# Keeping the loads of q, k, v and of layer one's raw weights in the source's order on the load queue

## The chip, the cores and the metric

The kernel runs on one core of a Trainium2 chip. The metric is the device time of one execution in microseconds (us); three timed runs of the kernel before are given, and one more execution was profiled. The engines are named as the profile names them: PE is the matrix engine (PEld its weight loads), ACT the scalar engine, DVE the vector engine, POOL GpSimd, and SPq the queue of the sync engine, on which this kernel issues all of its DMAs.

## The reference

Inputs are q, k and v in f32, 4 batches of 8 heads, 576 positions, 64 columns a head, and the weights of two layers in f64.

```python
scores = q @ k.T / sqrt(64)
Dmat   = where(i >= j, gamma[h] ** (i - j), 0)       # gamma = 1 - 2 ** (-5 - h)
x      = (scores * Dmat) @ v                          # heads side by side: 2304 x 512
h      = x @ w_in1                                    # 512 -> 2048
x      = where(h > 0, h, exp(min(h, 0)) - 1) @ w_out1 # 2048 -> 512
h      = maximum(x @ w_in2, 0)
out    = (h * h) @ w_out2
```

## The kernel before, in words

**Attention.** Because of the decay matrix the attention is computed as a recurrence over positions. The 2304 tokens are cut into chunks of at most 128 positions of one batch; chunk 0 to 3 make up the first token block, chunk 4 to 8 the second, 9 and 10 the third, 11 to 14 the fourth, 15 to 19 the fifth. A chunk has three loads on SPq, q, k and v (`load_chunk`, L204), a scaling of q and k (`scale_chunk`, L214, on POOL for the chunks of block 0 that are loaded first, on DVE otherwise) and three pieces of work: the transposes (L239, copied out by ACT on L244), the scores (L252, masked by DVE on L255), and the values (L267 with the state `st` of the chunk before, L271 with v, then L281 and L287 or L289 for the new state). Chunk 1 to 3 live in space that later belongs to weights; all others share two buffers for each of q, k and v. So the loads of chunk 6 wait until chunk 4 is done with its buffers, those of chunk 7 until chunk 5 is, and so on; k and v are free once the new state's matmuls (L281) have read them.

**Weights.** Both layers are computed in three matmuls for each product (L130 to L132), from a high and a low f32 part. A weight arrives as raw f64, 512 KB for each of the 32 units of a layer (a unit is one 128-wide slice of w_in or of w_out; L145 and L150 in `load_raw`). `to_f32` turns it into f32 with two ACT operations (L160, L161) and four of DVE (L162, L163, L164, L167); `split_w` makes the two parts (ACT L126, DVE L127). Layer one's raw tile lies in the space in which the split weight comes to lie, so each of the 32 units has a place of its own.

**Order in the source.** `load_next` for chunk 0 and 1, raw units 0 and 1, chunk 2 and 3. Then the pieces of chunk 0 to 3 in a written order, with `w1_to(n)` after each: it has n units split, n + 1 converted, and raw units asked for up to `AHEAD` beyond the converted ones. Chunk 4 is loaded after chunk 0's values, chunk 5 after chunk 2's. Then come the steps: step i multiplies one block by one slice of w_in (`up`), and two steps later by the slice of w_out (`down1`). Steps 0 to 5 belong to block 0, steps 6 to 11 to block 1. Each of the steps 0 to 4 first holds the three pieces of one of the chunks 4 to 8, and with a chunk's values the loads of the chunk two further on; then it calls `w1_to` with the limits 8, 9, 11, 12 and 14.

**Order on the engines.** The program isn't issued in the source's order. A list scheduler goes over all instructions with a simulated clock and issues on each engine what is ready first, earlier in the source before later among the ready. What an engine's list holds is fixed when the kernel is compiled, and each engine then works down its own list. A load of a raw unit of layer one is ready from the beginning, as soon as its place is free; a chunk's load is ready only when its buffers are free. In the same way a list can be tied: an issue-order edge says that one instruction of an engine stands behind another in its list, without a semaphore.

Of the kernel before, what the change touches and what calls it, by code (L numbers as in the profile page):

```python
# [18 lines left out]
P = 128  # L19
# [6 lines left out]
LAG = 2  # L26
WARM = 3

AHEAD = 6


GROUPS = ((0, 6), (6, 11), (11, 16))
# [66 lines left out]
def tile_kernel(ctx: ExitStack, tc, q, k, v, w_in1, w_out1, w_in2, w_out2, cst, out):  # L99
    nc = tc.nc  # L100
# [36 lines left out]
    def load_raw(layer, which, f):  # L137
        w = ((w_in1, w_out1), (w_in2, w_out2))[layer][which].bitcast(I32)
        if layer == 0:

            t = wp.tile([P, DM, 2], I32, tag=f"w{which}_{f}", name="raw")
        else:
            t = raw_p.tile([P, DM, 2], I32, tag="raw", name="raw")
        if which == 0:
            nc.sync.dma_start(  # L145
                out=t.rearrange("p (k f) t -> p k (f t)", k=KC),
                in_=w[:, 2 * f * P:2 * (f + 1) * P].rearrange("(k p) f -> p k f", p=P),
            )
        else:
            nc.sync.dma_start(out=t.rearrange("p c t -> p (c t)"), in_=w[f * P:(f + 1) * P, :])  # L150
        raws[layer, which, f] = t

    def to_f32(u):
# [38 lines left out]
    def load_chunk(ch):  # L192
        b, s, n = ch
        ts = []
        if ch in aside:
            tags = [f"w{i % 2}_{NF - 1 - 2 * aside.index(ch) - i // 2}" for i in range(4)]
            ts4 = [wp.tile([P, 2, DM], F32, tag=t, name="spare") for t in tags]
            spare[ch] = [t[:, i] for t in ts4 for i in range(2)]
        for i, (src, nm) in enumerate(((q, "q"), (k, "k"), (v, "v"))):
            if ch in aside:  # L200
                t = spare[ch][i].rearrange("s (h d) -> s h d", h=H)
            else:
                t = n_p.tile([P, H, D], F32, tag=nm, name=nm)
            nc.sync.dma_start(out=t[:n], in_=src[b, :, s:s + n, :].rearrange("h s d -> s h d"))  # L204
            ts.append(t)
        nat[ch] = ts

# [185 lines left out]
    def load_next():  # L393
        if at["load"] < len(chunks):
            load_chunk(chunks[at["load"]][0])
            at["load"] += 1
# [20 lines left out]
    def step(name, limit, todo_, work):  # L417
        if at[name] < min(limit, len(todo_)):
            work(todo_[at[name]])
            at[name] += 1  # L420
# [11 lines left out]
    def w1_run(n):  # L432
        while at["split"] < min(int(n), len(w1)):
            while at["raw"] < min(at["f32"] + AHEAD, len(w1)):
                step("raw", 99, w1, lambda u: load_raw(*u))
            step("split", at["f32"], w1, split_w)
            step("f32", at["raw"], w1, to_f32)
# [6 lines left out]
    for u in w1[:2]:  # L444
        load_raw(*u)
        at["raw"] += 1
# [17 lines left out]
    for i, (layer, blk, f) in enumerate(steps):  # L464
        def mid():
            for of, (lo, hi) in SPREAD.items():
                if lo <= i < hi:
                    need = 3 * len(blocks[of])
                    for _ in range((i - lo + 1) * need // (hi - lo) - (i - lo) * need // (hi - lo)):
                        attn_step()  # L470
            if at["split"] < len(w1):
                w1_to(units1(i))
            elif layer == 0 and i >= SHARED and at["f322"] < min(len(w2), units2(i)):

                step("park", at["f322"], w2, park_w)
                with tc.issue_after(mark[0]):
                    step("f322", at["raw2"], w2, to_f32)
                while at["raw2"] < min(len(w2), at["f322"] + 2):
                    step("raw2", 99, w2, lambda u: load_raw(*u))
# [19 lines left out]
        if (layer, f) == (0, 1) and blk == NB - 1 or (layer, f) == (1, LAG) and blk < NB - 1:  # L499
            n = blk + 1 if layer else 0  # L500
# [30 lines left out]
```

## Time and profile before

| what | us |
|---|---|
| median of three timed runs | 938.24 |
| lowest and highest of them | 931.86 and 939.58 |
| the profiled execution | 935.93 |
| its span, first to last instruction | 934.2 |
| granted PE clock, mean over the span | 0.982 |

The span is what the trace shows; 1.7 us of the profiled execution lie around it. The median of the timed runs is 2.3 us above the profiled execution. A share of busy time near 1 for PE does not say that its clock was full: the granted clock is a column of its own, 1.00 for 2.4 GHz and 0.50 for 1.2 GHz.

### The profile page before, as it was taken

The page shows a single profiled execution, that of the slowest core. Times are in us where ns is not written, and L with a number is a line of the kernel's source. Part 1 is how long each engine was busy: PE and PEld are TensorE (multiplying, and loading weights), DVE is VectorE, ACT ScalarE, POOL GpSimd, SP SyncE. Part 2 cuts the span into 40 slices and gives each one's busy share as a digit, 9 for nine tenths or more (in the row PEclk, how much of TensorE's full clock was granted, in tenths as well). Part 3 has the DMA queues.
Part 4 walks back from the last instruction along what each step waited for, and adds up shares of the span by engine and source line. Part 5 has one row for each costly group of instructions (what it writes and reads, how often), then busy time and mean ns, then how long its engine had stood idle before and what let it go on. Part 6 is the DMA issues. An engine that isn't in the chain of part 4 may idle for free.

```text
span 934.2 us, 12422 instructions
## 1 busy us (share of the span) xinstructions
PE 904.7 (97%) x4934; PEld 751.4 (80%) x4934; DVE 508.7 (54%) x890; ACT 422.7 (45%) x770; POOL 9.1 (1%) x12
## 2 busy tenths in 40 slices
PE   7897899999999999999999999999999999999997
PEld 5775788777788987888788888888888988888886
DVE  5886887787668788776787632222223332223222
ACT  3663577665555666555677532222222222222221
POOL 3000000000000000000000000000000000000000
PEclk9798899999999999999999999999999999999999
DMA  9994333102437757434844520010003030001001
GB/s 244 295 369 103 67 93 101 63 29 91 135 97 230 214 138 215 124 126 168 293 136 147 169 91 1 1 66 25 1 1 135 1 113 1 1 1 45 1 1 45
DMA packets 97081, 97.47 MB, mean 104 GB/s; under 512 B 59264, under 2 KB 77824, under 8 KB 96512
## 3 DMA queue, kind: packets, MB, share of 16 engines
q1 hardware_dynamic: 97024, 96.69, 34.2%
q8 instruction: 38, 0.62, 0.3%
q14 instruction: 19, 0.16, 0.0%
HBM read 69.94 MB, written 26.74 MB: 103 GB/s over the span
## 4 chain that ended last, share of the span: by engine, by line
PE 89%; SPq 3%; DMA 3%; DVE 2%; ACT 1%; issue 1%; DVEq 0%
PE h L130 14%; PE acc L130 14%; PE h L132 14%; PE h L131 14%; PE acc L131 14%; PE acc L132 13%; SPq L204 2%; PE ps_o L271 2%; PE ps_s L252 1%; PE ps_o L267 1%; PE ps_t L239 1%; DMA f<-w2s 1%; DMA k<-in_k_dram 1%; DMA raw<-in_moe_w_out_dram 1%; PE ps_u L281 1%
## 5 line engine op out<-in xcount | busy, mean ns | idle before, releaser
L130 PE MATMUL h<-x,w 128*128 128x512 f32 (+1 forms) x640 | 240.0, 376 | 3.9 <-DVE t L317 3.5
L132 PE MATMUL h<-x,w 128*128 128x512 f32 (+1 forms) x640 | 237.5, 371 | 0.0
L131 PE MATMUL h<-x,w 128*128 128x512 f32 (+1 forms) x640 | 237.5, 371 | 0.0
L321 DVE SCALAR_TENSOR_TENSOR t<-h,t 128x512 f32<-128x512 f32 (+1 forms) x80 | 51.0, 638 | 230.0 <-ACT t L319 230.0
L319 ACT ACTIVATE t<-h 128x512 f32<-128x512 f32 (+1 forms) x80 | 44.4, 555 | 237.2 <-PE h L132 237.2
L130 PEld LDWEIGHTS h<-x,w 128*128 128x128 f32 x640 | 121.9, 191 | 27.5 <-DVE t L317 4.1
L132 PEld LDWEIGHTS h<-x,w 128*128 128x128 f32 x640 | 121.8, 190 | 20.9 <-DVE w L127 0.2
L131 PEld LDWEIGHTS h<-x,w 128*128 128x128 f32 x640 | 122.0, 191 | 20.5
L126 ACT CAST g<-t 128x512 fp32r<-128x512 f32 (+1 forms) x160 | 92.5, 578 | 99.7 <-DVE t L321 52.1
L127 DVE TENSOR_TENSOR g<-t,g 128x512 fp32r<-128x512 f32 (+1 forms) x160 | 101.8, 636 | 64.5 <-ACT g L126 58.3
L131 PE MATMUL acc<-g,w 128*128 128x512 f32 (+1 forms) x320 | 118.3, 371 | 0.0
L132 PE MATMUL acc<-g,w 128*128 128x512 f32 (+1 forms) x320 | 117.0, 370 | 0.0
L130 PE MATMUL acc<-g,w 128*128 128x512 f32 (+1 forms) x320 | 114.0, 377 | 0.9 <-ACT w L126 0.9
L130 PE MATMUL acc<-w,g 128*128 128x512 f32 x288 | 112.2, 390 | 0.0
L131 PE MATMUL acc<-w,g 128*128 128x512 f32 x288 | 112.2, 390 | 0.0
L132 PE MATMUL acc<-w,g 128*128 128x512 f32 x288 | 111.6, 389 | 0.0
L312 ACT ACTIVATE t<-h 128x512 f32<-128x512 f32 (+1 forms) x80 | 44.4, 555 | 87.2 <-PE h L132 83.3
L316 DVE SCALAR_TENSOR_TENSOR t<-e,t 128x512 f32<-128x512 f32 (+1 forms) x80 | 50.8, 636 | 54.8 <-ACT t L314 54.7
L130 PEld LDWEIGHTS acc<-g,w 128*128 128x128 f32 x320 | 59.5, 188 | 12.5 <-ACT w L126 1.1
L132 PEld LDWEIGHTS acc<-g,w 128*128 128x128 f32 x320 | 60.2, 188 | 10.2
L131 PEld LDWEIGHTS acc<-g,w 128*128 128x128 f32 x320 | 60.3, 188 | 9.9 <-issue 0.2
L132 PEld LDWEIGHTS acc<-w,g 128*128 128x128 f32 x288 | 54.1, 188 | 11.4
(65 smaller groups left out, 933.0 us busy)
## 6 DMA issues: line engine op xcount, KB each, us to landing
raw<-in_moe_w_in_dram SPq DMA_DIRECT2D x32, 512.0 KB, 6.5
raw<-in_moe_w_out_dram SPq DMA_DIRECT2D x32, 512.0 KB, 6.0
x2s<-x SPq DMA_DIRECT2D x16, 512.0 KB, 4.0
w2s<-f SPq DMA_DIRECT2D x32, 256.0 KB, 2.3
x<-x2s SPq DMA_DIRECT2D x4, 2048.0 KB, 8.3
f<-w2s SPq DMA_DIRECT2D x32, 256.0 KB, 2.7
out_dram<-o SPq DMA_DIRECT2D x18, 256.0 KB, 2.3
parts<-part SPq DMA_DIRECT2D x8, 512.0 KB, 3.4
```

Source lines behind the costliest of these rows:

```text
L126: nc.scalar.copy(pair_hi, src)
L127: eng.tensor_tensor(out=pair_lo, in0=src, in1=pair_hi.bitcast(F32), op=ALU.subtract)
L130: nc.tensor.matmul(ps, l_hi, r_hi, start=first, stop=False)
L131: nc.tensor.matmul(ps, l_hi, r_lo, start=False, stop=False)
L132: nc.tensor.matmul(ps, l_lo, r_hi, start=False, stop=last)
L204: nc.sync.dma_start(out=t[:n], in_=src[b, :, s:s + n, :].rearrange("h s d -> s h d"))
L239: nc.tensor.transpose(ps[:, p, :n], t[:n, 2 * p:2 * p + 2, :].rearrange("s h d -> s (h d)"), ident[:n, :n])
L271: nc.tensor.matmul(ps[e * D:(e + 1) * D, p, :n], vn[:n, 2 * p + e, :], live[e][:n, p, :n], start=not s, stop=True, skip_group_check=True,)
L312: nc.scalar.activation(t, h, AF.Relu, scale=-1.0)
L316: nc.vector.scalar_tensor_tensor(out=t, in0=e, scalar=1.0, in1=t, op0=ALU.add, op1=ALU.mult)
L319: nc.scalar.activation(t, h, AF.Relu)
L321: nc.vector.scalar_tensor_tensor(out=t, in0=h, scalar=0.0, in1=t, op0=ALU.max, op1=ALU.mult)
```

## The change

Each load of q, k and v, and each load of a raw unit of layer one, gets an issue-order edge to the instruction that stands just before it in the source on the same queue, whatever that is (`tc.keep_in_program_order`; the edge carries no semaphore). The raw loads of layer two, the stores and the loads of parked values get none. `AHEAD` is 4 in place of 6, so that `w1_to(n)` asks for raw units up to n + 4 in place of n + 6.

```diff
-AHEAD = 6
+AHEAD = 4
...
         if which == 0:
-            nc.sync.dma_start(
+            i = nc.sync.dma_start(
                 out=t.rearrange("p (k f) t -> p k (f t)", k=KC),
...
         else:
-            nc.sync.dma_start(out=t.rearrange("p c t -> p (c t)"), in_=w[f * P:(f + 1) * P, :])
+            i = nc.sync.dma_start(out=t.rearrange("p c t -> p (c t)"), in_=w[f * P:(f + 1) * P, :])
+        if layer == 0:
+
+            tc.keep_in_program_order(i)
         raws[layer, which, f] = t
...
-            nc.sync.dma_start(out=t[:n], in_=src[b, :, s:s + n, :].rearrange("h s d -> s h d"))
+            tc.keep_in_program_order(
+                nc.sync.dma_start(out=t[:n], in_=src[b, :, s:s + n, :].rearrange("h s d -> s h d"))
+            )
```

## Rows read from the trace of the kernel before

**Rows 1.** The page's second part: busy tenths and granted clock in 40 slices.

```profile
PE   7897899999999999999999999999999999999997
...
PEclk9798899999999999999999999999999999999999
```

**Rows 2.** Windows: PE, PEld, DVE, ACT, POOL busy us; granted clock, DMA share, GB/s.

```profile
38.30:115.90 77.60, 66.63 (x471) 53.71 (x469) 62.28 (x116) 42.76 (x80) 0.00 (x0) 0.91 0.65 188
...
38.30:74.00 35.70, 32.72 (x211) 25.76 (x210) 31.30 (x59) 22.51 (x41) 0.00 (x0) 1.00 1.00 327
40.00:60.00 20.00, 18.75 (x126) 15.16 (x127) 19.10 (x38) 15.00 (x28) 0.00 (x0) 1.00 1.02 355
```

**Rows 3.** Timeline of PE, 46 to 123 us; in brackets idle us before and its releaser.

```profile
46.57 0.68 PE L271 MATMUL ps_o<-P,v 64*64 64x64 f32 x16
...
73.91 0.63 PE L239 MATMUL ps_t<-cs,q 128*128 128x128 f32 x4 [1.28 <-DVE q L214]
...
80.26 2.08 PE L267 MATMUL ps_o<-qT,st 128*128 128x128 f32 x8 [3.35 <-DVE P L255]
...
85.45 0.50 PE L130 MATMUL h<-x,w 128*128 128x512 f32 x1 [0.35 <-ACT w L126]
...
115.86 0.48 PE L130 MATMUL h<-x,w 128*128 128x512 f32 x1
...
122.58 0.50 PE L130 MATMUL h<-x,w 128*128 128x512 f32 x1
```

**Rows 4.** Timeline of DVE, 78 to 81 us.

```profile
78.92 0.69 DVE L214 TENSOR_TENSOR k<-k,cs 128x512 f32<-128x512 f32 x1 [1.58 <-DMA k<-in_k_dram]
79.53 1.28 DVE L255 TENSOR_TENSOR P<-ps_s,cs 128x512 f32<-128x512 f32 x2
```

**Rows 5.** The chain that ended last, in order of time, at 72 us.

```profile
72.03 6.87 DMA k<-in_k_dram
```

**Rows 6.** Timeline of SPq, 21 to 64 us: start and length of DMA issues.

```profile
21.13 0.73 SPq L204 DMA_DIRECT2D q<-in_q_dram  x1
...
25.01 1.69 SPq L145 DMA_DIRECT2D raw<-in_moe_w_in_dram  x1
...
39.66 0.79 SPq L150 DMA_DIRECT2D raw<-in_moe_w_out_dram  x1
...
59.96 1.25 SPq L145 DMA_DIRECT2D raw<-in_moe_w_in_dram  x1
61.31 2.27 SPq L204 DMA_DIRECT2D q<-in_q_dram  x1
63.68 3.66 SPq L204 DMA_DIRECT2D k<-in_k_dram  x1
```

**Rows 7.** Windows in which PE or its clock falls, columns as in rows 2.

```profile
80.00:85.00 5.00, 4.74 (x40) 4.43 (x40) 1.48 (x4) 0.70 (x2) 0.00 (x0) 0.50 0.00 0
...
90.00:110.00 20.00, 16.40 (x146) 13.54 (x143) 17.95 (x36) 8.71 (x18) 0.00 (x0) 0.83 0.32 66
280.00:285.00 5.00, 2.56 (x22) 2.37 (x23) 5.00 (x11) 1.31 (x3) 0.00 (x0) 0.81 0.86 273
455.00:465.00 10.00, 7.84 (x28) 6.02 (x27) 7.69 (x14) 6.20 (x11) 0.00 (x0) 0.83 0.74 246
```

**Rows 8.** Raw loads of L145 up to 75 us: us to landing.

```profile
DMA to landing us min/median/max: 5.1/9.2/12.0
```

**Rows 9.** Timeline of ACT: conversions of raw units 5 and 8 begin.

```profile
31.00 0.65 ACT L160 ACTIVATE raw<-raw 128x512 int32<-128x512 uint32 x1
...
47.57 0.68 ACT L160 ACTIVATE raw<-raw 128x512 int32<-128x512 uint32 x1
```

**Rows 10.** Waits of SPq up to 130 us: sum, times, longest.

```profile
SPq L204 <- PE ps_u L281: 27.8, 4, 9.0
```

**Rows 11.** The page's DMA issues: KB each, median us to landing, whole span.

```profile
raw<-in_moe_w_in_dram SPq DMA_DIRECT2D x32, 512.0 KB, 6.5
...
k<-in_k_dram SPq DMA_DIRECT2D x13, 256.0 KB, 4.5
```

## The prediction

> **What bounds the kernel now.** I read the slices of the page first, then windows of the span, then PE's timeline where a window was not full, and from there back over DVE to the load queue. PE is the bound on the whole; nearly every slice after the fifth is full and at full clock [rows 1]. What can move the time is therefore what PE loses, as idle time or by a low clock. It loses most between 38.3 us, where step 0 begins, and 115.9 us, where step 6 does: 77.6 - 66.6 = 11.0 us idle, and at a mean clock of 0.91 another 0.09 x 66.6 = 6.0 us [rows 2]. The change works on the loads of just this stretch, so 17 us are at stake.
>
> The largest single hole is a late load. PE waits 1.28 us for the scaling of chunk 6's q and 3.35 us for chunk 6's mask [rows 3]. The mask was not late by itself: DVE had it behind the scaling of chunk 7's k, and that waited for its DMA [rows 4], which was issued at 72.03 us and took 6.87 us [rows 5]. Why so late: chunk 4's values, the last that hold buffers for chunk 6, begin at 46.57 us and last 0.68 [rows 3], yet chunk 6's q goes out at 61.31 and its k at 63.68 us, because raw loads stand in front, 19 of them, the one at 39.66 us the first and the one at 59.96 us the last [rows 6]. They are 19 x 0.524 = 10 MB, and the DMA engines are full (share 1.00 up to 74 us [rows 2]). None of the 19 is wanted soon: they are the units from 12 on, and the conversion of unit 8 begins at 47.57 us [rows 9].
>
> **The change part by part.**
>
> *Chunk loads no longer behind the raw loads.* In the source chunk 6's loads follow chunk 4's values in step 0, and the raw units from 11 on follow them. So chunk 6's q and k go out when their buffers are free, some 14 us earlier, and chunk 7's when chunk 5's state is done, with few raw loads beside them (a k landed in 4.5 us in the median of the span [rows 11], against 6.87 here). Then DVE isn't held in L214, and the 1.28 and the 3.35 us go. The clock fell to 0.50 after this hole [rows 7]; that cost half of 4.74 us, 2.4 us, and goes with it. Sum: 7.0 us.
>
> *The rest of the stretch.* From 90 to 110 us PE loses 3.6 us idle and 0.17 x 16.4 = 2.8 us by the clock [rows 7]. Here chunk 7 and 8 go through their chains of transposes, copies, scores, mask and values with only steps 4 and 5 beside them, since steps 1 to 3 were used up while chunk 6 was waited for. With the loads on time each chunk lies beside its own step. That could bring back all 6.4 us or nothing; what is late next is DVE. It works 62.28 us of these 77.6. While it was fed, from 38.3 to 74 us, it was busy for 31.30 of 35.70 us (88%), and in its fullest 20 us for 19.10 (95.5%) [rows 2]. The same work at these rates takes 62.28 / 0.88 = 71.0 or 62.28 / 0.955 = 65.2 us, so the whole stretch can gain 6.6 to 12.4 us. I take a third of the 6.4, 2.1 us: 7.0 + 2.1 = 9.1 us is near the middle of what DVE allows.
>
> *Four units ahead.* Raw units 5 and 6 change places with chunk 4's loads, which held the queue from 21.13 to 25.01 us [rows 6]. So unit 5 goes out at 23 us; with the 9.2 us that raw loads took here [rows 8] it lands at 32.2, 1.2 us after its conversion began in the kernel before [rows 9]. The cost lies between 0 (DVE's backlog hides it, or the load is quicker with less beside it) and 1.2 us; I take 1.2. From unit 11 on the raw loads stand behind the loads of chunk 6 and later ones. `w1_to` asks for a unit 4 units before it is converted, at 1.4 units a step 2.9 steps; steps 0 to 3 took 85.45 - 38.3 = 47.2 us [rows 3], so the lead is some 30 us. The queue's longest wait for a chunk's buffers was 9.0 us [rows 10], with a landing of 9.2 us [rows 8] 18.2 us: covered. I cost it at nothing; without this cover it is the second rival.
>
> *Later stages.* After unit 31 the edges hold q, k and v behind stores and behind raw loads of layer two. A q that used to go out ahead of its k then stands beside it; DVE scales k after q anyway, which hides it. PE's losses at 280 to 285 us (2.44 us idle, 0.19 x 2.56 = 0.5 us by the clock) and at 455 to 465 us (2.16 us idle, 0.17 x 7.84 = 1.3 us) [rows 7] end with other waits than that for a chunk's load. But the scheduler draws up every list anew, so such a hole may vanish or come a second time: 3 us either way at the one, 3.5 at the other. I take 0.
>
> *Sum.* 935.9 (the profiled execution) - 7.0 - 2.1 + 1.2 = 928.0 us. The timed median, 938.24, is 2.3 us above the profiled execution and the lowest run 4.1 us below it; the mean of all four is 936.4, so I make no correction.
>
> *A rule that speaks against the change.* SPq stood for 27.8 us in four waits for a chunk's buffers [rows 10], and nothing was issued in them. The Trainium skill, "DMA: Bandwidth & Descriptors", section "Anatomy of one DMA — SWDGE (gpsimd) path", says that DMA engines don't wait on semaphores; the issuing sequencer waits before it dispatches. The trace agrees with it for this queue. By that rule a chunk load whose buffers aren't free would hold back each raw load behind it, and the sum would be the second rival's.
>
> **The rivals.** About 1% is what a measurement of this kernel can tell from no change: 9.4 us, or 928.9 us on the faster side.
>
> First, DVE takes the load's place: the loads come early, but PE next waits for the queue of conversions, scalings and masks. For it speaks that DVE was busy for 19.1 of 20 us [rows 2]; against it that PE still got 18.75 of these, and that DVE worked 1.48 of the 5 us after the hole [rows 7]. The gain is then DVE's lower bound less the late unit, 6.6 - 1.2 = 5.4 us, and less than that if a hole of 3 us comes later: 930.5 to 933.5, say 932 us.
>
> Second, on the slower side: the wait moves to the raw loads. The place is SPq in steps 1 to 4, where raw units from 11 on stand behind chunk 6 to 9. ACT's and DVE's lists are drawn up with simulated landing times; where these are too early, a conversion stands in front of masks and scalings and waits for its raw load. The price: three chunks, each with one raw load waited for by its whole landing, 6.5 us [rows 11], are 19.5 us, less the 7.9 that the change otherwise gives: 935.9 + 11.6, some 947 us. It decides from where the lead falls below 18.2 us, that is for steps under 18.2 / 2.9 = 6.3 us. Step 6 was nearly that short (122.58 - 115.86 = 6.7 us), steps 0 to 3 took 11.8 us each [rows 3]. Against it: no ACT operation waited for a raw load in this stretch before.
>
> Third, the order changes but nothing follows: chunk 7's k still waits for chunk 5's state, and if the pieces of chunk 5 keep their place, the hole only moves: 936 us.
>
> Fourth, more gain: the 17 us of the stretch less 2 us for copies that stay, and half of the 7.4 us lost at 280 and 455 us, 18.7 in all: 917 us.
>
> **How the numbers follow.** Forecast 0.47, spread over 921 to 934 us with two thirds below 928.9; more gain 0.14; DVE 0.13; no effect 0.06; slower 0.20. Faster by over 1%: 0.31 + 0.14 = 0.45. Within 1%: 0.16 + 0.13 + 0.06 = 0.35. Slower: 0.20. The range from 918 to 944 us leaves out half of the fourth rival and half of the second, 0.17; the likeliest case alone has 921 to 934 us.
>
> **What would show it.** On SPq, chunk 6's q soon after chunk 4's values and before raw unit 11, and the last raw units far later than 60 us. A DMA share well under 1.00 between 45 and 75 us. No wait of DVE L214 for q or k above 1 us, step 6 near 107 us, and a granted clock of 1.00 from 75 to 85 us. For the second rival, waits of ACT L160 for raw loads. The prediction is wrong if step 6 begins as late as before, or if it begins earlier and the time is given back in new holes after 200 us.

## The result, and the profile after

The changed kernel takes 925.33 us (median of 4 runs, 924.72 to 926.99), the kernel before 937.13 (4 runs, 931.86 to 939.58): a ratio of 0.9884, 95% interval 0.9839 to 0.993. A later series gave 926.67 (6 runs, 923.43 to 928.73) and a ratio of 0.9903, interval 0.9878 to 0.9929. The profiled execution took 924.95 us, of which the span is 923.2, so 11.0 us less than the span of before, 934.2.

The page, span, PE's slices with the granted clock, and the raw loads' row of the DMA issues, answers to [rows 1, 11]:

```profile
span 923.2 us, 12432 instructions
...
PE   7898999999999999999999999999999999999997
...
PEclk9899899999999999999999999999999999999999
...
raw<-in_moe_w_in_dram SPq DMA_DIRECT2D x32, 512.0 KB, 5.3
```

The clock's digits in the second and the fourth slice are one higher, the eight in the fifth stays. A raw load lands in 5.3 us in the median, not 6.5. Next the load queue, start and length of issues; it answers to [rows 6]. Lines have moved: L208 is the load of a chunk.

```profile
23.00 1.23 SPq L145 DMA_DIRECT2D raw<-in_moe_w_in_dram  x1
...
38.26 0.37 SPq L208 DMA_DIRECT2D q<-in_q_dram  x1
38.73 0.55 SPq L208 DMA_DIRECT2D k<-in_k_dram  x1
45.76 0.37 SPq L208 DMA_DIRECT2D v<-in_v_dram  x1
46.18 0.57 SPq L145 DMA_DIRECT2D raw<-in_moe_w_in_dram  x1
...
59.64 0.37 SPq L208 DMA_DIRECT2D k<-in_k_dram  x1
...
150.01 0.50 SPq L150 DMA_DIRECT2D raw<-in_moe_w_out_dram  x1
```

Chunk 6's q goes out at 38.26 us (61.31 before) and its k at 38.73 (63.68), ahead of raw unit 11 at 46.18; chunk 7's k goes out at 59.64 (72.03 before), and raw loads still go out at 150 us. PE's timeline, to hold against [rows 3]: chunk 4's matmuls with v, waits of chunk 5, transposes of chunk 6, its first values, chunk 8's passage, and the first matmul of step 8 (the prediction calls it step 6).

```profile
45.04 0.68 PE L276 MATMUL ps_o<-P,v 64*64 64x64 f32 x16
...
47.24 0.66 PE L244 MATMUL ps_t<-cs,k 128*128 128x128 f32 x4 [0.93 <-ACT qT L249]
48.57 2.09 PE L257 MATMUL ps_s<-qT,kT 64*128 64x128 f32 x16 [0.68 <-ACT kT L249]
...
67.13 0.60 PE L244 MATMUL ps_t<-cs,q 128*128 128x128 f32 x4
...
75.46 1.05 PE L272 MATMUL ps_o<-qT,st 128*128 128x128 f32 x8
...
91.24 0.44 PE L244 MATMUL ps_t<-cs,q 64*128 64x64 f32 x4 [0.74 <-DVE st L292]
91.87 0.46 PE L244 MATMUL ps_t<-cs,k 64*128 64x64 f32 x4 [0.20 <-DVE x L127]
92.79 0.68 PE L257 MATMUL ps_s<-qT,kT 64*64 64x64 f32 x16 [0.46 <-ACT kT L249]
94.11 1.97 PE L272 MATMUL ps_o<-qT,st 128*128 128x64 f32 x8 [0.64 <-DVE P L260]
...
108.55 0.50 PE L130 MATMUL h<-x,w 128*128 128x512 f32 x1
```

The q goes out 23.0 us earlier than before, and ahead of chunk 4's values. Chunk 4 is the last of its batch: it makes no new state, so its q and k are done with after its transposes, and only the load of v (45.76 us) waits for its values (45.04 + 0.68 us). The same transposes in the kernel before:

```profile
37.95 0.46 PE L239 MATMUL ps_t<-cs,q 64*128 64x64 f32 x4
...
39.00 0.46 PE L239 MATMUL ps_t<-cs,k 64*128 64x64 f32 x4
```

So there the q stood some 23 us behind the raw loads (61.31 - 38.4), not the 14 that the prediction counts from chunk 4's values.

Chunk 6's transposes begin 6.8 us earlier and wait for nothing, and its values, which stood 3.35 us for the mask, begin at 75.46 in place of 80.26 without a wait. The step that begins at 108.55 began at 115.86. Windows, columns as in [rows 2]:

```profile
37.62:108.59 70.97, 65.82 (x467) 53.38 (x465) 61.02 (x115) 41.78 (x78) 0.00 (x0) 0.93 0.48 129
37.62:67.10 29.48, 27.88 (x179) 22.24 (x178) 29.34 (x57) 20.04 (x37) 0.00 (x0) 0.94 0.47 118
...
40.00:60.00 20.00, 18.39 (x125) 14.70 (x124) 19.97 (x39) 14.41 (x27) 0.00 (x0) 0.91 0.38 98
50.00:55.00 5.00, 5.00 (x18) 3.95 (x17) 5.00 (x10) 1.58 (x4) 0.00 (x0) 0.68 0.17 38
...
80.00:85.00 5.00, 4.23 (x31) 3.09 (x30) 4.68 (x10) 3.82 (x8) 0.00 (x0) 1.00 0.94 285
90.00:110.00 20.00, 17.97 (x117) 14.70 (x116) 16.54 (x33) 11.56 (x24) 0.00 (x0) 0.83 0.71 197
95.00:100.00 5.00, 5.00 (x43) 4.38 (x43) 2.96 (x6) 2.83 (x6) 0.00 (x0) 0.50 0.27 56
```

The first row is the stretch that [rows 2] shows with 77.60 us: it takes 70.97. PE's idle time in it fell from 10.97 to 5.15 us, the loss by the clock from 6.0 to 0.07 x 65.82 = 4.6. The clock that was 0.50 from 80 to 85 us [rows 7] is 1.00 there. It falls in a new place: 0.68 from 50 to 55 us, right behind chunk 5's two waits shown above (1.61 us in sum), where it was 1.00 before [rows 2]; that costs 0.32 x 5.00 = 1.6 us. From 95 to 100 us it is 0.50, right behind the four short waits of chunk 8 (2.04 us in sum); this fall isn't new, the window from 90 to 110 us had 0.83 before too [rows 7]. DVE is busy for 29.34 of the first 29.48 us.

Where the 11.0 us are, then: step 0 begins 0.7 us earlier (37.66 for 38.34), the stretch is 6.6 us shorter, and 11.0 - 7.3 = 3.7 us come after it. Most of these last are not there in a second profile of the same kernel, below, and the 0.7 us can't be put down to the change: over the profiles of all kernels of this document step 0 begins anywhere from 34.62 to 38.87 us, and in the second profile of the changed kernel at 35.55.

### The profile page after: what moved, and what is told of

Read it like the earlier page. It is cut to its first block, busy times and chain, and to the rows that moved or that the text cites. A ratio compares the mean times of both kernels' runs of the same rounds, so it can differ in the third digit from the quotient of the medians.

```text
span 923.2 us, 12432 instructions
## 1 busy us (share of the span) xinstructions
PE 899.0 (97%) x4934; PEld 747.5 (81%) x4934; DVE 507.0 (55%) x890; ACT 421.7 (46%) x770; POOL 9.0 (1%) x12
## 4 chain that ended last, share of the span: by engine, by line
PE 91%; DVE 3%; DMA 2%; ACT 2%; issue 1%; SPq 1%; DVEq 0%
PE h L130 14%; PE acc L130 14%; PE acc L131 14%; PE h L132 14%; PE h L131 14%; PE acc L132 14%; PE ps_o L276 2%; PE ps_s L257 2%; PE ps_o L272 2%; PE ps_t L244 1%; DMA raw<-in_moe_w_in_dram 1%; SPq L208 1%; PE ps_u L286 1%; DVE f L167 1%; DMA part<-parts 0%
## 5 line engine op out<-in xcount | busy, mean ns | idle before, releaser
L131 PEld LDWEIGHTS acc<-g,w 128*128 128x128 f32 x320 | 60.3, 188 | 10.7 <-DVE g L127 0.7
```

What stands on the lines that cost most here:

```text
L131: nc.tensor.matmul(ps, l_hi, r_lo, start=False, stop=False)
```

## The experiments

Each ratio is to the kernel before, run on the same chip in the same series. A difference in us is one between medians.

**Edges without the four, the four without edges.** The first keeps all edges and six units ahead, the second only sets four.

```diff
-AHEAD = 4
+AHEAD = 6
```

> The edges as in the change, but six units asked for ahead, as before. If the order of the loads is what counts (the loads of q, k and v no longer behind 19 raw loads), this is as the change: 924 to 929 us, chunk 6's q issued before 45 us, no wait of DVE for a chunk's q or k over 1 us. If the smaller number of units ahead is what counts, it is near the kernel before, 934 to 939 us.

Measured: 929.49 us (6 runs, 928.26 to 931.59), ratio 0.992, interval 0.99 to 0.9939. Chunk 6's q goes out at 42.56 us.

```diff
-AHEAD = 6
+AHEAD = 4
```

> Four units asked for ahead, no edges. If the order of the loads is what counts, nothing keeps the scheduler from letting the raw loads pass: chunk 6's q is issued near 60 us again, the hole of PE near 77 us is there, 934 to 939 us. If the four units are what counts, 924 to 929 us.

Measured: 936.82 us (12 runs, 931.12 to 939.89), ratio 0.9994, interval 0.9971 to 1.0017. So it is the edges. Without them four units show no gain; with them six and four can't be told apart by the intervals of this series and of the change's own (0.9878 to 0.9929).

**Load times and lists taken apart.** The scheduler lays out each engine's list from the times at which it thinks loads land, so the change moves two things at once. In these two kernels the program is built twice; the order of each engine's instructions is read from one build and fixed in the other, instruction by instruction. First the lists of the change on PE, ACT, DVE and POOL, and the load queue's list of before:

```diff
+    lists = {e: new[e] for e in compute}
+    lists[E.SP] = late[E.SP]
+    nc, arrays, _ = build(inputs, before, lists)
```

> PE, ACT, DVE and POOL work down the lists of the changed kernel, instruction by instruction, but the load queue keeps the list of the kernel before, with 19 raw loads ahead of chunk 6's. If the time at which the chunks' loads go out is what counts, it is no faster than before and may be slower, since the new lists want chunk 6 and 7 earlier and have less work beside them: 934 to 946 us, with DVE or POOL waiting for q or k of chunk 6 and 7. If the new lists by themselves bring the gain and the loads' times don't matter, 924 to 929 us.

Measured: 950.03 us (6 runs, 946.54 to 951.94), ratio 1.0131, interval 1.0106 to 1.0156. PE's timeline, and two windows:

```profile
75.21 0.69 PE L277 MATMUL ps_o<-P,v 128*64 128x128 f32 x2 [18.08 <-DVE P L261]
```

```profile
38.00:70.00 32.00, 16.55 (x83) 13.21 (x81) 9.80 (x20) 9.12 (x18) 0.00 (x0) 0.67 1.02 340
70.00:75.00 5.00, 0.00 (x0) 0.00 (x0) 1.74 (x3) 0.00 (x0) 0.00 (x0) 0.50 0.98 231
```

Chunk 6's q and k go out at 62.65 and 65.02 us here, as late as before. DVE's list has their scaling early; while DVE waits for them it does nothing else (9.80 us of work in 32), and PE stands for 18.08 us.

Then the other way: the lists of before on the four engines, and loads of chunks 0 to 10 and raw loads in the source's order, four units ahead.

```diff
+    _, _, old = build(inputs, before)
+    nc, arrays, _ = build(inputs, (4, True, range(11)), {e: old[e] for e in compute})
```

> The reverse: PE, ACT, DVE and POOL work down the lists of the kernel before, and the loads of chunk 0 to 10 and of layer one's raw weights are in the source's order, four units ahead; later loads are free. If the loads' times count by themselves, the hole near 77 us (3.35 us for the mask, 1.28 for q, 2.4 by the clock) goes and nothing else changes: 928 to 932 us. If the new lists are needed, 934 to 939 us.

Measured: 933.95 us (12 runs, 931.09 to 936.09), ratio 0.9969, interval 0.995 to 0.9987. Its timelines of SPq, DVE and PE, and its window from step 0 to step 8:

```profile
38.17 0.37 SPq L208 DMA_DIRECT2D q<-in_q_dram  x1
```

```profile
71.91 0.68 DVE L220 TENSOR_TENSOR q<-q,cs 128x512 f32<-128x512 f32 x1
```

```profile
72.74 0.63 PE L245 MATMUL ps_t<-cs,q 128*128 128x128 f32 x4 [1.27 <-DVE q L220]
...
76.52 0.71 PE L273 MATMUL ps_o<-qT,st 128*128 128x128 f32 x4 [0.78 <-DVE P L261]
...
89.56 1.16 PE L273 MATMUL ps_o<-qT,st 128*128 128x128 f32 x8 [1.40 <-DVE P L261]
...
97.70 1.62 PE L273 MATMUL ps_o<-qT,st 128*128 128x64 f32 x7 [1.90 <-DVE P L261]
```

```profile
34.62:112.02 77.40, 66.23 (x470) 52.91 (x469) 62.90 (x118) 42.23 (x79) 0.00 (x0) 0.93 0.49 129
```

The q is asked for at 38.17 us, but DVE scales it at 71.91, because that is its place on DVE's list. The 3.35 us for the mask fell to 0.78; the 1.28 us for the q are still there (1.27), and so are later waits. By the medians early loads alone are worth 2.4 us of 936.3 and the new lists alone cost 13.7. In the profile the early loads don't even shorten the stretch: from step 0 to step 8 it takes 77.40 us (77.52 before), with 11.2 us of it idle on PE (11.0 before), and the 3.8 us by which step 8 begins earlier lie almost wholly ahead of step 0. The change's gain needs both, and the lists hold the larger part of it, but only because the loads are there.

**The change again, and each of its kinds of edges alone.** A second series has the change itself:

> The changed kernel itself once more, as a measure for the other runs of the same chip: 924 to 928 us.

Measured: 926.67 us, given above. Its profiled span is 925.3 us, 2.1 longer than in the first profile. Step 8 begins at 107.82 us, so 8.0 us earlier than before of 8.9 in all; only 0.9 us come after it. Of the 8.0 us, 2.8 lie ahead of step 0 (35.55 us) and 5.2 in the stretch. What the two profiles of this one kernel differ in is a hole at 450 us. In the second profile, PE's timeline and a window:

```profile
451.77 0.50 PE L130 MATMUL h<-x,w 128*128 128x512 f32 x1 [2.92 <-DVE t L322]
```

```profile
450.00:460.00 10.00, 8.23 (x29) 6.62 (x30) 7.73 (x13) 6.14 (x12) 0.00 (x0) 0.83 0.81 288
```

The same two views of the first profile:

```profile
451.25 0.50 PE L130 MATMUL h<-x,w 128*128 128x512 f32 x1 [1.51 <-DVE t L322]
```

```profile
450.00:460.00 10.00, 8.75 (x38) 7.24 (x39) 7.23 (x12) 5.75 (x11) 0.00 (x0) 1.00 0.84 279
```

The same wait is 1.41 us longer in the second, and the clock of the ten us around it 0.83, not 1.00: 0.17 x 8.23 = 1.4 us more. That is 2.8 of the 3.7 us that the first profile gained after step 8.

Only the raw loads of layer one keep their order, four units ahead; the chunk loads have no edges:

```diff
-            tc.keep_in_program_order(
-                nc.sync.dma_start(out=t[:n], in_=src[b, :, s:s + n, :].rearrange("h s d -> s h d"))
-            )
+            nc.sync.dma_start(out=t[:n], in_=src[b, :, s:s + n, :].rearrange("h s d -> s h d"))
```

> Four units ahead and the edges on layer one's raw loads alone; the loads of q, k and v are free. Up to the loads of chunk 9 the lists of all engines are those of the change, after that they differ. If the whole gain comes from the stretch up to step 8, as the prediction has it (later stages 0), this is as the change, 924 to 928 us. If about 4 us of it come from the later stages, as the trace of the changed kernel has it (idle and clock at 280 and 455 us), 928 to 932 us.

Measured: 925.7 us (9 runs, 923.91 to 932.37), ratio 0.9922, interval 0.9893 to 0.995; step 6 begins at 96.85 us, in the change at 96.91 (same series). Only the loads of chunks from 9 on keep their order; the raw loads and chunks 0 to 8 have no edges:

```diff
-        if layer == 0:
-            tc.keep_in_program_order(i)
...
+            if at["load"] >= 9:
+                tc.keep_in_program_order(i)
```

> Four units ahead and the edges on the loads of q, k and v of chunk 9 and later alone; raw loads and earlier chunks are free, so that 19 raw loads stand in front of chunk 6's as before, while the lists of the later stages are those of the change. If the later stages bring nothing, 934 to 939 us, as before. If they bring about 4 us, 930 to 934 us.

Measured: 934.21 us (12 runs, 932.07 to 936.66), ratio 0.9984, interval 0.9966 to 1.0002. Window and waits (sum, times, longest) of this kernel:

```profile
70.00:90.00 20.00, 13.09 (x89) 10.68 (x88) 11.17 (x21) 5.85 (x11) 0.00 (x0) 0.74 0.64 145
```

```profile
DVE q L218 <- DMA q<-in_q_dram: 6.7, 3, 4.7
```

The hole of before is there in full. So what counts is that each raw load stays behind the instruction that stands before it in the source, which for unit 11 is chunk 6's load of v; a chunk load then finds the queue free without an edge of its own. By the interval, edges on the late chunks give between 3.2 us (0.34% of 935) and nothing.

**Three units ahead**, with all edges.

```diff
-AHEAD = 4
+AHEAD = 3
```

> The change with three units asked for ahead. By the prediction's reckoning the lead is 3 / 1.4 = 2.1 steps of some 10 us, 21 us, against 18.2 us of the longest wait with a landing: still covered, 924 to 929 us, no longer waits of ACT for raw loads than in the changed kernel (2.2 us in two). If the raw loads are what runs short with fewer units ahead (the second rival), ACT waits longer for them and the time is 930 us or more.

Measured: 929.52 us (7 runs, 928.39 to 932.48), ratio 0.9948, interval 0.9925 to 0.9971, 2.85 us above the change; step 6 begins at 101.94 us. Its waits from 20 to 130 us that end with a DMA, all of them, and the window of steps 0 to 4:

```profile
DVE q L218 <- DMA q<-in_q_dram: 2.4, 2, 2.0
POOL spare L218 <- DMA spare<-in_q_dram: 2.2, 1, 2.2
DVE k L218 <- DMA k<-in_k_dram: 0.2, 1, 0.2
```

```profile
37.60:70.00 32.40, 27.88 (x190) 21.86 (x187) 27.65 (x53) 18.41 (x33) 0.00 (x0) 0.94 0.35 85
```

No conversion waits for a raw load even here. PE has 27.88 us of work in this window; in the change, same series, 30.79. What makes three units slower stays open.

**Chunk loads on another queue.** To tell a place in SP's queue from full DMA engines, the kernel before sends loads from chunk 6 on from ACT's queue.

```diff
-            nc.sync.dma_start(out=t[:n], in_=src[b, :, s:s + n, :].rearrange("h s d -> s h d"))
+            eng = nc.sync if at["load"] < 6 else nc.scalar
+            eng.dma_start(out=t[:n], in_=src[b, :, s:s + n, :].rearrange("h s d -> s h d"))
```

> The kernel before, with no edges and six ahead, but the loads of chunk 6 and later are issued on ACT's queue instead of SPq, so that no raw load stands in front of them in the list; the raw loads still fill the DMA engines up to some 70 us. If the place in SPq's list is what made chunk 6's and 7's loads late, they go out when their buffers are free and the time is near the change, 925 to 930 us, unless ACT's own list holds them. If the full DMA engines are what makes them late, they land late all the same: 933 to 939 us.

Measured: 961.81 us (5 runs, 960.31 to 963.83), ratio 1.0284, interval 1.0264 to 1.0303. A piece of the chain that ended last; from ACT's timeline the issue of chunk 6's q and the next operation; a window:

```profile
52.94 8.81 DMA raw<-in_moe_w_out_dram
```

```profile
61.83 0.42 ACTq L205 DMA_DIRECT2D q<-in_q_dram  x1
62.34 0.62 ACT L126 CAST w<-f 128x512 fp32r<-128x512 f32 x1 [25.87 <-DMA raw<-in_moe_w_out_dram]
```

```profile
50.00:62.00 12.00, 0.00 (x0) 0.00 (x0) 0.00 (x0) 0.00 (x0) 0.00 (x0) 0.50 1.06 382
```

The q waits on ACT as long as it did on SP (61.83 and 61.31 us), now with ACT behind it. Why is in the program's own lists, with the counters on which each DMA waits (SP's lines first, then ACT's; the number ahead is the place in the list):

```
43 L150 DMA raw_1671<-in_moe_w_out_dram 128x1024 [waits DMAHW2_49]
...
50 L145 DMA raw_1097<-in_moe_w_in_dram 128x4x256 [waits DMAHW1_49,PE_49,Pool_49]
51 L150 DMA raw_1250<-in_moe_w_out_dram 128x1024 [waits DMAHW3_49]

29 L205 DMA q_526<-in_q_dram 128x8x64 [waits DMAHW2_49,DVE_49]
```

In this part of the program DMAs take eight counters in turn, in the order in which the scheduler places them, and each waits for the one that had its counter eight places before. Chunk 6's q is placed between SP's 50th and 51st, so it waits for the 43rd, a raw load. Here another queue didn't take the load out from behind the raw loads, since its place in the scheduler's order stayed behind them. That raw load took 8.81 us on full engines (share 1.06). So the run settles what held the q, not what the q would have cost had it been issued early beside the same raw loads.

The Trainium skill, "DMA: Bandwidth & Descriptors", section "Anatomy of one DMA — SWDGE (gpsimd) path", says that DMA engines don't wait on semaphores and that the issuing sequencer waits before it dispatches. This run agrees, though not on the path that the section is about: ACT did nothing for 25.87 us, and the issue at 61.83 us stands at their end.

**Is DVE what is late next?** DVE is full up to chunk 6, so I moved the scaling of q and k of chunks 4 to 8 to POOL, in the kernel before, in the change, and in the kernel that orders raw loads alone.

```diff
-        eng = nc.gpsimd if ch in blocks[0] else nc.vector
+        eng = nc.gpsimd if ch in blocks[0] + blocks[1] else nc.vector
```

> The kernel before, with the scaling of chunk 4 to 8 on POOL instead of DVE. The loads stay late, but DVE's masks no longer stand behind a scaling that waits for its load. If DVE's place in line is what turned the late k of chunk 7 into PE's 3.35 us, about that and the clock after it come back: 929 to 934 us. If the late load itself is on the chain of chunk 7 anyway, 934 to 939 us.

Measured: 934.96 us (12 runs, 931.71 to 939.47), ratio 1.0003, interval 0.9984 to 1.0022. Timeline of POOL:

```profile
42.13 4.03 POOL L214 TENSOR_TENSOR q<-q,cs 128x512 f32<-128x512 f32 x1 [8.60 <-DMA q<-in_q_dram]
...
71.31 1.39 POOL L214 TENSOR_TENSOR q<-q,cs 128x512 f32<-128x512 f32 x1 [23.96 <-DMA q<-in_q_dram]
```

Masks no longer stand behind a late k (3.35 us fell to 0.78), and yet the time is the same: the load is as late as it was, and POOL waits for it 23.96 us.

> The changed kernel with the scaling of chunk 4 to 8 on POOL. DVE loses ten operations of 0.68 us in the stretch in which it works 61 of 71 us. If DVE is what bounds the stretch after the change, as the first rival has it, 919 to 924 us; if the chunks' chains or the copies on ACT are, 924 to 928 us. POOL takes 1.04 us for what DVE does in 0.68, and DVE operations beside POOL's took up to 1.5 us in the kernel before, so 930 us is possible too.

Measured: 931.33 us (12 runs, 927.56 to 935.22), ratio 0.9959, interval 0.9942 to 0.9975: 4.7 us above the change of the series before it (whose kernel before had the same median, 935.05 and 935.04). PE's two longest waits from 38 to 110 us, sum, times and longest:

```profile
PE ps_o L272 <- DVE P L260: 2.6, 2, 1.8
PE h L130 <- DVE t L322: 2.5, 1, 2.5
```

> The same scaling on POOL with the edges on layer one's raw loads alone, four units ahead: 919 to 924 us if DVE is the bound after the change, else 923 to 928 us, as that variant without POOL.

Measured: 931.88 us (12 runs, 926.61 to 935.81), ratio 0.9962, interval 0.9942 to 0.9983, 6.2 us above the same kernel without POOL. Relieving DVE in this way loses. It can't say what DVE's share costs, since the scaling itself is slower on POOL (1.04 to 1.71 us, once 4.03; DVE's takes 0.69 [rows 4]) and every list is drawn up anew.

## Why the prediction was right, and where its steps were not

**The sum.** The forecast was 7.9 us less than 935.9 us, 928.0; the medians are 925.33 and 926.67. Up to step 8 the profiles have 7.3 and 8.0 us, in all 11.0 and 8.9. That these lie so close is in part luck. For the stretch itself the terms say 7.0 + 2.1 = 9.1 us, and it gave 6.6 in the first profile and 5.2 in the second; what is missing there came from ahead of step 0 (0.7 and 2.8 us, where I had put a loss of 1.2) and from after step 8.

**The late load and its hole (7.0 us).** The load went out ahead of raw unit 11 as I named, both waits of PE are gone, the clock is 1.00 from 75 to 85 us, and chunk 6's first values begin 4.8 us earlier (75.46 for 80.26). Three things in the term were not so. The load went out 23.0 us earlier and not 14: I read chunk 4's values as the last work that holds chunk 6's buffers, which is true of v alone. Of the clock's 2.4 us, 1.6 are lost again behind chunk 5. And the reason was half of it. I wrote that "DVE isn't held in L214, and the 1.28 and the 3.35 us go", as if the lists stayed. With the lists of before the early loads gave 2.4 us by the medians, about a third of the term, the 1.28 us stayed, and the stretch was no shorter. The rest is the scheduler moving chunk 6's pieces forward once it sees the load land early. I had that sentence only for the later stages ("the scheduler draws up every list anew"), where I used it as noise.

**The rest of the stretch (2.1 us).** Between 90 and 110 us I named 6.4 us and took a third of it. PE's idle time there fell from 3.6 to 2.0 us, but the loss by the clock, 2.8 us [rows 7], is 0.17 x 17.97 = 3.1 now, so some 1.3 us came back here (the window holds work that is some 7 us further on). Chunk 8 still passes with four waits, and the clock falls behind it.

**The steps.** I called the matmuls at 85.45 us step 4 and those at 115.86 step 6. Steps 0 and 1 run interleaved from 38.34 on, and 6 and 7 from 104.74 on: 85.45 is step 5 and 115.86 step 8. "Step 6 near 107" was thus said of step 8, which begins at 108.55 us (107.82 in the second profile). Steps 0 to 4 took 9.4 us each, not 11.8, and the lead of 2.9 steps was 27 us, not some 30; it was still enough.

**Four units ahead (1.2 us, taken for unit 5).** The wait is there, its price isn't. Unit 5's load goes out at 23.00 us, and ACT waits for it:

```profile
31.73 0.67 ACT L163 ACTIVATE raw<-raw 128x512 int32<-128x512 uint32 x1 [0.91 <-DMA raw<-in_moe_w_in_dram]
```

The conversion begins 0.7 us later than before [rows 9], and in the second profile, after a wait of 2.72 us, 1.0 later. Nothing on PE is later for it: right behind this conversion ACT stands another 4.28 us for PE (1.06 in the second), and step 0 begins earlier in both. In the whole span ACT waits 2.2 us for raw loads, 1.3 at the longest. I priced four units as a cost and left out what they might save; with edges, six gives 929.49 and four 926.67 in different series, which isn't settled, and three is 2.85 us slower than four.

**Later stages (0).** Right, though the first profile hides it: 3.7 us there, 0.9 in the second, and the difference is one wait at 450 us that is longer in one execution than in another. The edges on late chunks alone are worth 0.8 us by the medians, with an interval that takes in 0.

**The rivals.** The second, a wait that moves to the raw loads, didn't come, with four units or with three. The third is what the change would be without its edges (0.9994). The rule of the Trainium skill that spoke against the change was true of the queue, whose wait for ps_u rose from 27.8 us to 36.0 up to 130 us (the longest from 9.0 to 12.2), and cost nothing, since raw loads had a lead of 27 us. For the first, DVE was busy for 99.5% of the time up to chunk 6's transposes, but over the stretch for 61.02 of 70.97 us (86%). The gain is larger than the 5.4 us that I gave this rival, and of PE's waits in the stretch that are left, 1.5 us end with DVE and 3.5 with ACT; whether DVE sets what is left stays open. The fourth's 7.4 us at 280 and 455 us are 6.4 by the figures given for the later stages (2.44 + 0.5 + 2.16 + 1.3), so it stood for 918 us rather than 917; 11.0 of its 18.2 us came in the first profile.

## What to carry to other kernels

Where a scheduler draws up the lists from simulated landing times, an edge that holds back loads nobody wants soon acts twice, by the earlier load and by the lists that follow from it; cost both, since the one without the other gave 2.4 us and cost 13.7 us here. Find the loads that stand in front of the wanted one and order those: edges on the raw loads alone, each to the load before it in the source, gave as much as all edges. Moving the late load to another engine's queue put that engine behind it for 26 us, as its wait on an earlier raw load went with it.

## What the runs showed of the hardware

- Waits of PE under 1 us each were followed by the lower clock. In the changed kernel two waits of 1.61 us in sum at 46 to 49 us were followed by 0.68 over five us, and four of 2.04 us in sum at 91 to 94 us by 0.50. Around one wait of 2.92 us at 450 us the clock was 0.83 over ten us, and around one of 1.51 it was 1.00, in two executions of one kernel. I can't say from these rows which property decides.
- The same elementwise product of 128x512 took POOL from 1.04 to 4.03 us in one kernel (the kernel before with the scaling of chunks 4 to 8 on POOL), where DVE takes 0.69 [rows 4].
- With the DMA engines at a share of 1.06, 512 KB loads issued from 50 to 66 us in the kernel that loads from ACT's queue took 10.7 to 11.1 us to land in the median; from 45 to 75 us of the changed kernel, at a share of 0.29, 4.6 to 5.0.
